# A new written-out order and three deeper rings in a fused retention and SoLU kernel

## The chip, the core and the metric

The kernel runs on one core of a Trainium2 chip. The metric is the device time of one execution in microseconds, and smaller is better. The kernel before took 209.02 us (median of three runs, 208.08 to 209.44). One further execution was recorded by the profiler; every duration below comes from it.

The core has five engines, each with its own queue that works strictly in order: TensorE (PE, matrix products and transposes), VectorE (DVE), ScalarE (ACT), GpSimd (POOL) and SyncE (SP, which here only issues transfers). They wait for each other through semaphores.

## What is computed

```
scores = (1/8) * q @ k^T                        # 8 batches, 8 heads, 576 positions, 64 wide
Dmat   = gamma[h] ** (i - j) where i >= j, else 0   # gamma[h] = 1 - 2**(-5-h)
ret    = (scores * Dmat) @ v
x      = ret, heads side by side                # 4608 tokens x 512
h      = x @ w_in                               # 512 -> 1024
u      = h * softmax(h)
ln     = (u - mean(u)) / sqrt(var(u) + 1e-6) * g_ln
out    = ln @ w_out                             # 1024 -> 512
```

All inputs and the output are float32; the products are taken in float16 with float32 sums.

## The kernel before

**Tiling.** Positions are cut into chunks of 128 tokens. A unit is a pair of chunks of one batch, loaded together (units 0 to 3, 5 to 8 and so on), or the two 64-token tails of two batches (units 4, 9, 14, 19). There are 20 units and 36 chunks. Within a unit the retention is computed directly; across chunks a 64 x 64 state per head is carried, decayed by `gamma ** 128`. The last chunk (35) is worked in two halves, `35.0` and `35.1`.

**Steps.** Each step of the work is a small function with a name, and one list, `PLAN`, writes out all of them in order. A word such as `xT:4@s` is step `xT` for chunk 4 on engine `s` (ACT; `v` is DVE, `g` is POOL), and `TL:2/05` is step `TL` for unit 2 into PSUM banks 0 and 5. `follow(PLAN)` issues the instructions word by word; so the list sets the order on every engine, and data and buffer conflicts only add waits. There are eight PSUM banks, and a bank may be written again when its reader is done.

The steps, by engine:

- SP: `lq`, `lk`, `lv` load a unit (512 KB each, 256 KB for the tails in two transfers); `wi`, `wo` load a quarter of `w_in` or `w_out`; `mt` a mask; `dT` transposes a chunk's `u` by a transfer; `st` stores a chunk.
- POOL: `q` and `v` scale by decay tables and cast; `s32` decays the state; `w2`, `pow` end the variance; and `k`, `s16`, `ws`, `osb`, `cwA`, `cwB` where the list says `g`.
- PE: `TL` transposes q and k of a unit, `sc` the scores, `kp` the state update, `xs` and `xv` the two parts of the retention's output, `mm1` and `mm2` the two dense products, `TU` and `lp` turn `u` where `dT` doesn't, `mean` a column mean of the scaled `w_out`; `tick` and `warm` are filler products on zeros.
- DVE: `m` masks scores, `max` and `solu` the row maximum and `u`, `t` the state, `cw` the centred `w_out`, `ox` a correction of the first six chunks; and copies where the list says `v`.
- ACT: `exp`, `sq` (the sum of squares), `w1`; and copies where the list says `s`.
- Copies out of PSUM: `eX` and `eY` (q and k turned), `eU`, `uX`, `uY` (`u` turned), `xT` (the retention's output turned and cast), `osb` (the scaled result).

**Order of the dependences.** Per unit: `lq`, `lk` -> `q`, `k` -> `TL` -> `eX`, `eY` -> `sc` -> `m` -> `xv` (with `v`) -> `xT`. Per chunk: `xT` -> `mm1` -> `max` -> `exp` -> `solu` -> (`sq`, and `dT` or `TU`) -> `mm2` -> `osb` -> `st`. Every `mm2` needs the scaled weights: `wo` -> `ws` for chunks 0 to 5, which use `w_raw16`, and `ws` -> `mean` -> `cw` for the rest, which use `w_out16`.

**Rings.** Buffers are used in turn, chunk n taking place n modulo the depth: `LB` = 3 units of loads, `XB` places for `xT`, `EB` for `e`, `UB` for `u`, `OB` for results, `UTB` for `u` turned by `dT` (chunks 10 to 33). Some places lie in room that has had its first use: the float32 copy of `w_out`, `w_out32`, which `ws` and `cw` read, holds the `dT` places.

```
ut_ = [w_out32[:, i].bitcast(F16).rearrange("p (c m) -> p c m", m=P) for i in range(UTB)]
o_sb = ring(min(OB, 5), [DM], FP, "o_sb")
o_sb += [w_out32[:, 6]] * (OB - len(o_sb))
u_ += [w_out32[:, 7].bitcast(F16)] * (UB - len(u_))
```

Ahead of `follow` the kernel loads the small tables on ACT's queue, writes zeros, ones, the identity and triangles, and builds two masks of 128 x 1024, the first on DVE and the second on POOL (both at line 865).

Of the kernel before, what the change touches and what calls it, by code (L numbers as in the profile page):

```python
# [43 lines left out]
def kernel(  # L44
# [690 lines left out]
    def warm(k, j, eng, bk):  # L735
# [26 lines left out]
        sc:4.0/01 exp:6 t:9 mm1:7/34 m:4.0 s32:9 lv:7 sq:5 lk:8 solu:6 q:6.0 lv:9 TU:2/01  # L762
        s16:5.0@s xv:4.0/2 eU:2.0@s t:10 q:6.1 lq:8 sc:5.0/67 xs:8/2 m:5.0 eU:2.1@s pow:0
        TL:6/50 xT:8@s max:7 q:7.1 eY:6@s sc:5.1/12 mm1:8/67 m:5.1 s16:9.0@g exp:7 s16:9.1@g
        osb:1@g eX:6@s solu:7 xv:5.1/10 xv:5.0/10 k:7.1@g xs:10/0 xT:9@s osb:0@g max:8
        sc:6.1/45 xT:10@s sc:6.0/12 k:7.0@g s16:10.0@s xs:12/3 mm2:2/0 m:6.0 sq:4 q:7.0 st:0
        st:1 k:8.0@g m:6.1 lk:10 sq:7 mm1:9/12 lk:9 v:8.1 ox:2 exp:8 lq:10 v:7.1 lq:9
        xv:6.1/03 osb:2@s max:9 xv:6.0/03 q:8.0 mm2:4/4 xT:12@s xT:11@s solu:8 s32:10 st:2
        exp:9 TU:3/03 ox:4 s16:10.1@g sq:8 mm1:10/67 v:9.0 solu:9 k:8.1@s v:8.0 lv:12 eU:3.0@v
        sq:6 TL:7/24 max:10 v:7.0 mm1:11/01 w1:3 sq:9 eU:3.1@v q:8.1 eX:7@v eY:7@s k:10.1@g  # L770
        lq:11 max:11 kp:7/23 kp:8/23 exp:10 lv:10 w2:3 mm2:5/5 k:9.0@g t:13 w1:6 lk:12 solu:10
        s16:13.0@s w2:6 lk:11 q:9.0 exp:11 TL:8/24 lv:11 ox:5 mm1:12/67 s32:13 lq:12 solu:11
        w1:9 eY:8@s q:10.1 eX:8@s t:14 sc:7.0/45 TU:4/01 m:7.0 s16:13.1@g mm2:6/3 eU:4.1@s
        pow:3 max:12 sq:11 q:10.0 sc:7.1/45 eU:4.0@v pow:6 xs:13/2 exp:12 mm2:7/1 m:7.1
        osb:5@g k:12.0@s k:10.0@g solu:12 osb:6@s osb:4@g xv:7.1/20 xv:7.0/20 sc:8.0/45
        osb:7@v osb:3@g xT:13@s sc:8.1/67 xs:14/0 m:8.1 mm1:13/23 xT:14@s st:4 sq:10 st:5 st:3
        m:8.0 lk:13 k:12.1@s TL:9/10 st:6 w2:9 TL:10/76 eX:9@v eY:9@s dT:11 q:11.0 xv:8.0/45
        eX:10@v sq:12 xv:8.1/45 mm1:14/01 max:13 q:12.0 dT:12 k:11.1@s v:12.0 exp:13 xs:15/4
        st:7 xs:16/5 max:14 mm2:8/7 v:10.1 dT:10 s16:14.1@s xT:15@v xT:16@s s16:14.0@g exp:14
        solu:13 mm1:15/45 q:12.1 eY:10@s solu:14 v:11.1 osb:8@s TL:12/23 max:15 pow:9  # L780
        sc:9.0/01 eX:12@s mm1:16/67 v:11.0 st:8 m:9.0 k:11.0@s lq:15 eY:12@s q:11.1 xv:9.0/0
        max:16 exp:15 sc:10.0/12 v:10.0 lq:14 xs:17/0 mm2:11/3 m:10.0 exp:16 lv:13 lq:13
        solu:15 xT:17@s dT:13 kp:11/21 kp:10/21 sq:14 t:18 sc:10.1/45 mm2:10/0 m:10.1 osb:11@s
        s32:18 sq:13 solu:16 s16:18.0@g st:11 TL:11/23 osb:10@s dT:15 xv:10.1/45 t:19 w1:12
        xv:10.0/45 eY:11@s sc:12.1/67 w2:12 eX:11@v mm1:17/01 s16:18.1@g lk:15 xT:18@s m:12.1
        s16:19.1@g sq:15 st:10 sc:11.0/67 max:17 sc:11.1/34 mm2:9/2 q:13.0 lk:14 m:11.1 exp:17
        k:13.0@g dT:14 m:11.0 xs:19/5 mm1:18/34 s16:19.0@g xT:19@s v:13.0 osb:9@s solu:17
        lv:14 k:13.1@s pow:12 xv:11.0/67 max:18 xv:11.1/67 mm1:19/01 q:14.0 st:9 exp:18 q:13.1
        xs:21/7 mm2:12/2 max:19 xT:21@s v:12.1 xT:20@s solu:18 v:13.1 exp:19 mm1:20/67
        k:15.1@g lv:16 osb:12@s solu:19 dT:16 k:14.0@g sq:16 TL:13/25 max:20 sc:12.0/01 st:12  # L790
        eX:13@s q:15.1 mm1:21/34 lq:17 m:12.0 lv:15 exp:20 v:14.0 eY:13@v xs:22/1 w1:15 sq:17
        mm2:14/0 max:21 w2:15 solu:20 exp:21 mm2:13/2 q:15.0 osb:14@v k:15.0@g solu:21 pow:15
        TL:15/60 osb:13@s st:14 xv:12.1/17 s32:19 eY:15@v xv:12.0/17 dT:18 sc:13.0/23 xT:22@s
        eX:15@v kp:13/45 sq:18 kp:12/45 m:13.0 sc:13.1/01 st:13 mm2:15/6 dT:17 sq:21 t:22
        m:13.1 s16:22.1@g lk:16 w1:18 mm1:22/23 sq:20 lk:17 s16:22.0@g osb:15@v dT:19 s32:22
        xs:23/7 xs:25/1 max:22 v:15.0 xT:23@s xv:13.1/41 st:15 xv:13.0/41 xs:24/4 mm1:23/67
        q:17.1 xT:25@v exp:22 t:23 v:16.1 xT:24@v sq:19 mm2:16/5 max:23 q:17.0 solu:22 v:16.0
        exp:23 mm1:24/01 dT:20 k:16.1@g osb:16@s solu:23 w2:18 sq:22 lq:16 mm1:25/34 k:16.0@g
        max:24 pow:18 st:16 lq:18 v:15.1 exp:24 mm2:17/2 max:25 k:17.0@g s16:23.1@g solu:24
        exp:25 kp:16/56 k:17.1@g kp:15/56 mm2:18/7 s16:23.0@g t:27 osb:17@s sq:23 solu:25  # L800
        s16:27.1@g s32:27 st:17 TL:17/02 osb:18@v TL:14/31 eX:17@s sc:15.1/45 t:28 q:16.1
        mm2:19/7 m:15.1 eX:14@s st:18 q:16.0 eY:14@s lk:18 s16:27.0@s eY:17@v sc:15.0/56 dT:23
        sc:14.0/34 m:15.0 TL:16/12 mm2:20/0 eY:16@s q:18.1 dT:22 eX:16@v osb:19@s m:14.0 lv:17
        sc:17.0/67 osb:20@s xv:15.1/15 xv:15.0/15 sc:16.0/23 xT:27@s xv:14.0/4 m:16.0 xs:26/4
        k:18.1@g sq:25 xs:28/5 st:20 mm1:27/01 dT:21 m:17.0 w1:21 xT:26@s w2:21 sq:24 q:18.0
        lv:18 mm1:26/23 max:27 lk:19 xT:28@s s32:28 exp:27 mm2:23/4 pow:21 max:26 solu:27
        exp:26 v:17.0 mm1:28/67 k:18.0@g osb:23@s solu:26 v:17.1 TL:18/05 max:28 sc:17.1/34
# [95 lines left out]
```

## Time and profile before

| | |
|---|---|
| median of three runs | 209.02 us |
| the profiled execution | 206.33 us, of which the span of its instructions is 204.6 us |
| busy share of the span | PE 96%, DVE 84%, ACT 79%, POOL 69% |
| transfers | 48.83 MB, 239 GB/s on average |
| PE filler (`warm`) | 56 products of 512 columns, 16.1 us busy |

An engine's busy time is the union of its instructions, without the issuing of transfers and without waits. PE's products are pipelined: one of 512 columns is shown as some 379 ns long, while the next may start sooner. PEld is PE's loading of the stationary operand, which overlaps with products. A row of groups reads: line, engine, operation, out<-in, shapes, count | busy us, mean ns of one | idle time before, and what ended it. A row of the timeline or of the chain begins with the start in us from the beginning of the span and the length. Lines are those of the kernel: L152 and L154 are the helper behind all copies, L195 that behind `q` and `v`, L467 that of all wide products, L227 of all transposes on PE, L345 is `sc`, L373 `kp`, L416 `xv`, L399 `xs`.

### The profile page before, as it was taken

How to read it: one execution, taken by the hardware profiler on the slowest of the kernel's cores; microseconds unless marked ns; L12 is line 12 of the kernel's file. 1: busy time of each engine (PE TensorE's matmuls, PEld its weight loads, DVE VectorE, ACT ScalarE, POOL GpSimd, SP SyncE). 2: the span in 40 equal slices, each digit the busy share in tenths (PEclk: the TensorE clock that was granted, in tenths of full speed). 3: DMA queues.
4: the chain of work that ended last, by engine and by line, in shares of the span. 5: the costliest groups of instructions: out<-in, count | busy, mean ns of one | idle time of the engine just before them, and what ended most of it. 6: DMA issues, size and time to landing. Idle time of an engine off the chain costs nothing.

```text
span 204.6 us, 7473 instructions
## 1 busy us (share of the span) xinstructions
PE 196.2 (96%) x3156; PEld 104.5 (51%) x3156; DVE 172.7 (84%) x225; ACT 162.0 (79%) x282; POOL 142.0 (69%) x196
## 2 busy tenths in 40 slices
...
GB/s 131 288 319 379 318 341 313 248 282 234 263 287 283 263 230 301 306 268 232 201 231 234 240 217 278 236 216 292 252 242 248 202 192 57 193 185 81 205 139 117
DMA packets 96369, 48.83 MB, mean 239 GB/s; under 512 B 40784, under 2 KB 90320, under 8 KB 96336
## 3 DMA queue, kind: packets, MB, share of 16 engines
...
q14 instruction: 9, 0.07, 0.1%
...
## 4 chain that ended last, share of the span: by engine, by line
PE 61%; POOL 9%; DMA 8%; DVE 8%; SPq 6%; ACT 4%; issue 3%; POOLq 0%; DVEq 0%; ACTq 0%
PE ps L467 47%; DMA qf<-in_q_dram 6%; SPq L174 4%; PE ps L345 4%; PE ps L416 3%; PE ps L227 3%; POOL v L195 3%; DMA w_out<-u 3%; PE ps L399 2%; POOL w_raw L704 2%; POOL q L195 2%; DVE w_out L722 2%; DVE u L539 2%; PE ps L373 2%; SPq L672 1%
## 5 line engine op out<-in xcount | busy, mean ns | idle before, releaser
L467 PE MATMUL ps<-w_in,xT 128*128 128x512 f16 x288 | 67.2, 379 | 0.3 <-DVE u L539 0.3
L496 DVE TENSOR_REDUCE col_nm<-ps 128x1 f32<-128x1024 f32 (+1 forms) x37 | 44.1, 1193 | 6.2 <-PE ps L467 5.9
L506 ACT ACTIVATE e<-ps,col_nm 128x1024 f32<-128x1024 f32 (+1 forms) x37 | 40.4, 1092 | 9.8 <-DVE col_nm L496 9.0
L539 DVE SCALAR_TENSOR_TENSOR u<-ps,e 128x1024 f16<-128x1024 f32 (+1 forms) x37 | 43.9, 1190 | 3.1 <-ACT e L506 1.7
L467 PE MATMUL ps<-w_out,w_out 128*128 128x512 f16 x192 | 44.9, 380 | 0.0
L467 PEld LDWEIGHTS <-xT 128*128 128x128 f16 x288 | 26.7, 98 | 30.8 <-ACT xT L152 0.3
L195 POOL TENSOR_TENSOR q<-qf,small 128x512 f16<-128x512 f32 x36 | 37.4, 1048 | 7.0 <-DMA qf<-in_q_dram 4.9
L547 ACT ACTIVATE e<-u,col_su 128x1024 f32<-128x1024 f16 (+1 forms) x37 | 41.5, 1124 | 0.0
L195 POOL TENSOR_TENSOR v<-vf,small 128x512 f16<-128x512 f32 x36 | 37.2, 1048 | 4.9 <-DMA vf<-in_v_dram 4.8
L355 DVE TENSOR_TENSOR ret<-ps,masks 128x1024 f16<-128x1024 f32 x22 | 26.5, 1218 | 9.0 <-PE ps L345 8.9
L467 PEld LDWEIGHTS <-w_out 128*128 128x128 f16 x192 | 17.8, 98 | 19.6
L152 ACT COPY tt<-ps 128x1024 f16<-128x1024 f16 (+1 forms) x23 | 20.6, 921 | 3.2 <-PE ps L227 2.2
L152 ACT CAST xT<-ps 128x512 f16<-128x512 f32 x28 | 15.9, 584 | 7.9 <-PE ps L399 4.9
L556 POOL TENSOR_SCALAR col_w<-col_ss 128x3 f32<-128x3 f32 (+1 forms) x14 | 2.7, 196 | 27.2 <-ACT col_w L533 13.4
L737 PE MATMUL ps<-zeros 128*128 128x512 f16 x56 | 16.1, 431 | 0.8 <-ACT tu L152 0.8
L154 POOL CAST s<-t 64x512 f16<-64x512 f32 x20 | 12.1, 608 | 4.8 <-DVE t L433 3.9
L446 POOL TENSOR_TENSOR s<-t,small 128x512 f32<-128x512 f32 x12 | 12.5, 1044 | 3.7 <-DVE t L431 3.5
L648 DVE TENSOR_SCALAR o_sb<-ps,col_rs 128x512 f32<-128x512 f32 (+1 forms) x14 | 10.0, 711 | 5.2 <-PE ps L467 2.7
L152 ACT CAST k<-kf 128x512 f16<-128x512 f32 x15 | 9.1, 621 | 6.3 <-DMA kf<-in_k_dram 6.3
L154 POOL CAST k<-kf 128x512 f16<-128x512 f32 x21 | 12.7, 611 | 1.6 <-DMA kf<-in_k_dram 1.6
L652 ACT ACTIVATE o_sb<-ps,col_rs 128x512 f32<-128x512 f32 x17 | 11.6, 685 | 1.4 <-PE ps L467 1.2
L355 DVE TENSOR_TENSOR w_in<-ps,masks 128x1024 f16<-128x1024 f32 x10 | 12.0, 1215 | 0.0
...
## 6 DMA issues: line engine op xcount, KB each, us to landing
...
out_dram<-o_sb SPq DMA_DIRECT2D x32, 256.0 KB, 3.4
...
qf<-in_q_dram SPq DMA_DIRECT2D x8, 128.0 KB, 4.2
kf<-in_k_dram SPq DMA_DIRECT2D x8, 128.0 KB, 4.7
```

The source lines that it names most:

```text
L152: nc.scalar.copy(out=out, in_=in_)
L154: {"v": nc.vector, "g": nc.gpsimd}[eng].tensor_copy(out=out, in_=in_)
L195: nc.gpsimd.tensor_tensor(out=out, in0=in_, in1=table.unsqueeze(2).to_broadcast([P, H, D]), op=ALU.mult)
L355: nc.vector.tensor_tensor(out=ret[u % RB][:, s], in0=bank(b0, 1024).rearrange("p (h w) -> p h w", w=P), in1=mk, op=ALU.mult,)
L446: nc.gpsimd.tensor_tensor(out=st32[c % 2].rearrange(flat), in0=T_OF[n].rearrange(flat), in1=gs2.unsqueeze(2).to_broadcast([P, 8, D]), op=A ...
L467: nc.tensor.matmul(out=o, lhsT=lhs(slice(0, P)), rhs=rhs, start=start, stop=stop)
L496: nc.vector.tensor_reduce(out=col("nm", n, j), in_=h(n, j), axis=AX.X, op=ALU.max, negate=True)
L506: nc.scalar.activation(out=e_[n % EB][:, part(j)], in_=h(n, j), func=ACT.Exp, bias=col("nm", n), accum_out=col("s", n, j),)
L539: nc.vector.scalar_tensor_tensor(out=u_[n % UB][:, part(j)], in0=h(n, j), scalar=1.0, in1=e_[n % EB][:, part(j)], op0=ALU.mult, op1=ALU.mu ...
L547: nc.scalar.activation(out=e_[n % EB][:, part(j)], in_=u_[n % UB][:, part(j)], func=ACT.Square, bias=col("su", n), scale=-1.0 * DFF, accum ...
L652: nc.scalar.activation(out=dst, in_=o, func=ACT.Copy, scale=col("rs", n))
L737: nc.tensor.matmul(out=bank(bk[0]), lhsT=zeros[:, 0:P], rhs=zeros, start=True, stop=True)
```

## The change

Four things change. First, the rings: `XB` goes from 3 to 5, `OB` from 5 to 6 and `UTB` from 4 to 6; `UB` stays 6, but one of its places moves into `w_out32[:, 7]`, and the sixth result place is `w_out32[:, 6]`. Second, seven tables `gn` that no step reads are left out of `small`. Third, the second mask is built on DVE instead of POOL. Fourth, `PLAN` is a new list: the same steps apart from filler (`tick` 12 to 6, `warm` 56 products to 52), in another order on every engine and in the transfer queue, with other banks, and with copies moved between engines. Counted over both lists:

| copies | ACT | DVE | POOL |
|---|---|---|---|
| `xT` | 28 to 23 | 8 to 13 | |
| `eX`, `eY` | 28 to 28 | 12 to 12 | |
| `eU` | 8 to 10 | 4 to 2 | |
| `osb` | 18 to 17 | 14 to 15 | 5 to 5 |
| `uX`, `uY` | 3 to 1 | 1 to 3 | |
| `ws` | 2 to 4 | | 6 to 4 |
| `k` | 15 to 16 | | 21 to 20 |
| `s16` | 12 to 13 | | 20 to 19 |

The transfer queue begins, before and after:

```
lq0 lk0 lq1 lv1 lk1 lv0 wi3 wi0 wi2 wi1 lk2 lq2 wo1 lq3 lk3 wo0 wo3 wo2 lv2 lv3
wi0 lq1 lk1 lq0 lk0 lv1 lv0 wi2 wi1 wi3 wo0 wo3 lq2 wo2 lk2 wo1 lq3 lk3 lv2 lv3
```

The diff, with most of both lists left out:

```diff
@@ -30,8 +30,7 @@
     gs = ge ** 128.0
 
     gm = np.broadcast_to((g ** -128.0).reshape(4, 2).T.reshape(1, 8), (P, 8))
-    gn = [ge ** float(2**i) for i in range(7)]
-    return np.concatenate([gq, gqt, gv, gvt, gs, gs, gm] + gn, axis=1).astype(np.float32)
+    return np.concatenate([gq, gqt, gv, gvt, gs, gs, gm], axis=1).astype(np.float32)
 
 
 def _np_tail_mask():
@@ -84,12 +83,12 @@
         return chunks[units[u]][1] == 4
 
 
-    LB, QB, KB, TB, WB, RB, XB, EB, UB, OB, TQ, UTB = 3, 2, 4, 4, 3, 3, 3, 4, 6, 5, 2, 4
+    LB, QB, KB, TB, WB, RB, XB, EB, UB, OB, TQ, UTB = 3, 2, 4, 4, 3, 3, 5, 4, 6, 6, 2, 6
 
     def ring(count, shape, dtype, name):
         return [const.tile([P] + shape, dtype, name=f"{name}{i}") for i in range(count)]
 
-    small = const.tile([P, 92], FP, name="small")
+    small = const.tile([P, 64], FP, name="small")
     tris = const.tile([P, 3, 64], FP, name="tris")
     masks = const.tile([P, 2, H, P], FP, name="masks")
     mask_t = const.tile([P, P], FP, name="mask_t")
@@ -124,7 +123,7 @@
     st32 = ring(2, [2, 4, D], FP, "s32_")
     xT_ = ring(XB, [4, P], F16, "xT")
     e_ = ring(EB, [DFF], FP, "e")
-    u_ = ring(min(UB, 6), [DFF], F16, "u")
+    u_ = ring(min(UB, 5), [DFF], F16, "u")
 
     ut_ = [w_out32[:, i].bitcast(F16).rearrange("p (c m) -> p c m", m=P) for i in range(UTB)]
     o_sb = ring(min(OB, 5), [DM], FP, "o_sb")
@@ -740,90 +739,89 @@
 
 
     PLAN = """
-        lq:0 lk:0 lq:1 lv:1 lk:1 tick:12/4 warm:18/4 lv:0 q:0.0 wi:3 q:0.1 k:0.0@s k:0.1@s
-        TL:0/62 wi:0 warm:8/4 q:1.1 eX:0@s eY:0@s wi:2 v:1.0 sc:0.0/01 sc:0.1/67 warm:9/4
-        m:0.1 q:1.0 wi:1 k:1.1@s m:0.0 v:1.1 k:1.0@s TL:1/67 lk:2 warm:5/4 v:0.1 eX:1@v eY:1@v
-        lq:2 v:0.0 sc:1.1/12 cwA:3@s kp:1/63 m:1.1 cwB:3@g kp:0/63 wo:1 xv:0.1/50 warm:1/4
-        cwA:0@s cwB:0@g t:0 sc:1.0/12 xv:0.0/50 warm:7/4 m:1.0 lq:3 s16:0.1@s cwB:2@s cwA:2@g
-        xT:0@v s16:0.0@s lk:3 xv:1.0/15 xv:1.1/15 cwB:1@s cwA:1@g xs:1/0 xT:2@v xs:3/5 s32:0
-        xT:1@s mm1:0/67 wo:0 g32 t:1 k:2.1@g mm1:1/12 s32:1 max:0 xT:3@s wo:3 s16:1.1@s
-        k:2.0@s q:2.1 mm1:3/34 exp:0 max:1 wo:2 q:2.0 solu:0 exp:1 ws:2@g TL:2/05 lv:2 max:3
-        eX:2@s mm1:2/67 ws:3@g eY:2@s solu:1 q:3.1 lv:3 warm:2/0 exp:3 max:2 q:3.0 TU:0/25
-        sc:2.1/01 lq:4 eU:0.1@s s16:1.0@g solu:3 k:3.1@g k:3.0@s warm:1/5 lk:5 exp:2 ws:0@g
-        m:2.1 TL:3/35 warm:2/4 ws:7@g eX:3@s solu:2 sc:2.0/01 lk:4 warm:3/4 eY:3@s ws:6@g
-        m:2.0 TU:1/34 ws:4@s ws:5@g sc:3.0/67 lq:5 ws:1@s eU:1.0@v sc:3.1/01 xs:4/5 v:2.1
-        m:3.1 eU:0.0@s mean/3 eU:1.1@s v:2.0 m:3.0 mm2:0/1 evm cw:4 v:3.1 sq:3 cw:2 v:3.0
-        kp:2/42 sq:1 ox:0 xv:3.1/67 xv:2.1/50 xv:2.0/50 cw:0 q:4.0 lv:6 kp:3/42 sq:0 xv:3.0/67
-        lk:6 xs:6/6 t:4 mm2:3/1 lv:5 cw:3 s16:4.1@g s16:4.0@s lv:4 cw:5 xT:4@s s32:4 xT:6@s
-        cw:7 xs:7/7 mt:0 xs:5/0 sq:2 mm1:4/45 k:5.0@g ox:3 k:4.0@g cw:1 xT:5@s q:5.1 lq:6
-        k:5.1@s t:5 mm1:5/01 xT:7@s max:4 q:5.0 w1:0 lk:7 v:6.1 cw:6 exp:4 TL:5/62 max:5
-        mm2:1/3 s16:5.1@g eX:5@s v:6.0 solu:4 lq:7 exp:5 mm1:6/67 k:6.0@g ox:1 eY:5@s v:5.1
-        solu:5 k:6.1@s TL:4/34 v:5.0 max:6 kp:6/25 eY:4@s eX:4@s w2:0 lv:8 kp:5/25 v:4.0
...
-        pow:34 mm2:32/6 exp:35.0 solu:35.1 pow:33 osb:30@s solu:35.0 sadd:35 w1:35 TU:5/02
-        osb:32@v lp:35.1/47 lp:35.0/35 eU:5.0@s mm2:33/1 suadd:35 st:32 eU:5.1@s uY:35.0@v
-        st:30 uX:35.1@s sq:35.0 mm2:34/5 sq:35.1 osb:33@v uX:35.0@s st:33 ssadd:35 uY:35.1@s
-        w2:35 mm2:35.0/2 pow:35 osb:34@v mm2:35.1/3 st:34 osb:35.0@v st:35.0 osb:35.1@v
-        st:35.1
+        wi:0 lq:1 tick:6/1 warm:28/1 lk:1 lq:0 lk:0 lv:1 lv:0 q:1.0 wi:2 k:1.0@s q:1.1 k:1.1@s
+        wi:1 TL:1/56 warm:8/1 q:0.1 eX:1@s eY:1@s cwB:0@g wi:3 cwA:0@g k:0.0@s sc:1.0/56 q:0.0
+        warm:5/1 k:0.1@s m:1.0 wo:0 v:1.0 sc:1.1/67 TL:0/50 m:1.1 warm:5/1 eX:0@s v:1.1 wo:3
+        eY:0@v v:0.0 sc:0.1/56 sc:0.0/34 lq:2 warm:4/7 m:0.1 v:0.1 cwA:2@s m:0.0 kp:1/52 wo:2
+        cwB:2@g kp:0/52 warm:2/7 g32 cwA:1@s t:0 xv:1.1/31 cwB:1@s xv:0.0/06 lk:2 xv:1.0/31
+        s16:0.1@s s16:0.0@g xv:0.1/06 xT:2@v cwB:3@s cwA:3@g xs:3/1 xT:0@v xs:1/6 wo:1 s32:0
+        mm1:2/45 ws:0@s ws:1@g t:1 xT:1@s lq:3 mm1:0/23 max:2 ws:6@s xT:3@s lk:3 exp:2
+        mm1:1/01 max:0 q:2.0 s16:1.0@s lv:2 q:2.1 solu:2 mm1:3/67 ws:4@s ws:5@g exp:0 max:1
+        lv:3 k:2.0@s k:2.1@g max:3 exp:1 ws:7@g TL:2/45 lq:5 solu:0 ws:3@g ws:2@s exp:3 solu:1
+        s32:1 lk:5 mean/3 eX:2@s solu:3 s16:1.1@g eY:2@s q:3.0 lk:4 TU:0/14 cw:4 eU:0.1@s
+        q:3.1 eU:0.0@v TU:1/52 sc:2.0/67 cw:0 sc:2.1/01 sq:3 k:3.0@g lq:4 mm2:0/4 m:2.0
+        k:3.1@g evm v:2.1 cw:1 eU:1.0@s TL:3/76 m:2.1 v:2.0 mm2:1/5 eX:3@s ox:0 lv:5 eY:3@s
+        v:3.1 cw:7 xs:4/4 eU:1.1@s ox:1 v:3.0 sc:3.0/67 xv:2.0/41 xv:2.1/41 m:3.0 xT:4@s q:5.0
+        lv:6 kp:2/20 kp:3/20 sq:0 sc:3.1/45 lk:6 cw:6 mm1:4/67 lv:4 t:4 k:5.0@s k:5.1@g m:3.1
+        s16:4.1@s s16:4.0@g lq:6 sq:2 s32:4 xs:5/1 mm2:3/2 max:4 xT:5@s q:4.0 cw:3 w1:0 exp:4
+        xs:6/5 t:5 xs:7/4 q:5.1 lq:7 xv:3.1/54 cw:2 sq:1 xv:3.0/54 mm1:5/01 s16:5.0@g solu:4
+        mt:0 xT:7@s v:5.0 xT:6@s cw:5 sq:4 v:5.1 mm1:6/67 max:5 lq:8 v:6.1 k:4.0@s ox:3 exp:5
+        lk:7 max:6 k:6.0@g TL:4/23 mm1:7/45 k:6.1@g eY:4@s solu:5 v:6.0 exp:6 lv:8 s16:5.1@g
+        eX:4@v TL:5/10 sq:5 solu:6 w2:0 kp:6/23 kp:5/23 q:6.0 eX:5@s t:9 sc:4.0/67 v:4.0 m:4.0
+        eY:5@s TU:2/12 q:6.1 eU:2.0@s max:7 xv:4.0/0 sc:5.0/67 xs:8/0 s32:9 lq:9 m:5.0 xT:8@s
+        exp:7 TL:6/01 s16:9.1@g lk:8 t:10 mm1:8/67 lv:9 q:7.1 eY:6@s solu:7 lv:7 pow:0
+        eU:2.1@s sc:5.1/34 k:7.1@g max:8 mm2:2/5 s16:9.0@s k:7.0@g eX:6@s q:8.1 m:5.1 exp:8
+        TU:3/10 osb:0@g ox:2 sc:6.0/34 eU:3.0@s q:7.0 m:6.0 xv:5.0/25 xv:5.1/25 xs:10/5 st:0
...
+        sq:12 mm2:11/2 eX:11@v dT:14 v:10.1 m:10.1 exp:16 mm2:10/0 v:12.1 eY:11@s solu:16
...
+        lq:16 v:16.0 solu:22 mm1:25/67 sq:20 dT:20 v:14.0 max:23 mm1:24/12 k:17.1@g max:25
...
+        osb:22@s solu:27 s16:31.1@s s16:31.0@g t:32 TL:18/56 q:19.0 dT:27 sc:17.1/01 eX:18@v
...
+        xT:33@v xT:34@s solu:29 s16:32.1@s mm2:26/3 w1:27 s16:32.0@s max:30 dT:29 sq:29
...
+        solu:33 dT:31 sq:30 mm1:34/01 max:32 st:25 eY:19@s exp:32 mm2:28/2 max:34 solu:32
...
+        mm2:31/5 eU:5.0@v xT:35@s w2:33 st:27 eU:5.1@s pow:30 mm1:35.0/0 st:29 dT:30
+        mm1:35.1/7 osb:31@s max:35.0 mm2:32/6 st:28 max:35.1 st:31 nmm:35 exp:35.0 mm2:33/4
+        exp:35.1 osb:32@v solu:35.0 sadd:35 st:32 pow:33 w1:35 solu:35.1 mm2:34/5 w2:34
+        osb:33@v pow:34 suadd:35 st:33 sq:35.0 lp:35.0/62 lp:35.1/40 osb:34@v sq:35.1 mm2:30/1
+        uX:35.0@v st:34 uY:35.0@s uY:35.1@v ssadd:35 uX:35.1@v w2:35 pow:35 mm2:35.1/3
+        osb:30@s mm2:35.0/0 st:30 osb:35.1@v st:35.1 osb:35.0@v st:35.0
...
             )
 
         make_mask(nc.vector, masks[:, 0], tris[:, 1:3], P)
-        make_mask(nc.gpsimd, masks[:, 1], tris[:, 0:2], P)
+        make_mask(nc.vector, masks[:, 1], tris[:, 0:2], P)
         follow(PLAN)
```

109 lines of the change are left out of this document (49 added, 60 removed).

## The prediction

> **What bounds the kernel now.** I read the page first, then busy time by stage, then the chain of waits, and last the rows of single operations.
>
> ```profile
> span 204.6 us, 7473 instructions
> PE 196.2 (96%) x3156; PEld 104.5 (51%) x3156; DVE 172.7 (84%) x225; ACT 162.0 (79%) x282; POOL 142.0 (69%) x196
> ```
>
> The profiled execution took 206.33 us, 1.7 around its span; the median of the runs, 209.02, is 2.7 above that. Three engines are near full, so the stages have to tell them apart (columns: window, wall time, then PE, PEld, DVE, ACT, POOL busy).
>
> ```profile
> 0.00:22.00 22.00, 19.81 (x325) 10.16 (x326) 10.50 (x15) 9.18 (x14) 15.45 (x25) 1.00 1.00 280
> 22.00:42.00 20.00, 18.58 (x384) 10.15 (x382) 18.09 (x23) 18.32 (x28) 18.96 (x21) 1.00 1.07 304
> 42.00:148.00 106.00, 105.08 (x1864) 56.87 (x1866) 101.28 (x129) 93.96 (x162) 87.54 (x115) 1.00 1.07 254
> 148.00:176.00 28.00, 27.94 (x433) 15.13 (x422) 25.08 (x31) 23.42 (x43) 14.37 (x22) 1.00 0.91 190
> 176.00:201.00 25.00, 24.76 (x173) 12.20 (x170) 17.40 (x30) 17.17 (x39) 5.63 (x15) 1.00 0.67 156
> ```
>
> Up to 22 us the loads rule (PE is busy there mostly with filler on zeros). From 22 to 42 DVE, ACT and POOL are each over 90% busy. From 42 to 148 DVE is idle 4.7 of 106 us and PE 0.9. After 176 DVE has 7.6 us to spare and PE none. The chain of waits gives PE's true pace (start, length, what):
>
> ```profile
> 12.86 11.95 DMA qf<-in_q_dram
> ...
> 66.60 0.57 PE ps L416 x32
> ...
> 73.92 0.71 PE ps L373 x64
> 74.63 1.83 PE ps L467 x8
> 76.46 0.57 PE ps L227 x32
> 77.04 1.83 PE ps L467 x8
> 78.87 0.35 PE ps L345 x16
> ...
> 130.29 8.63 PE ps L467 x40
> ...
> 195.45 5.32 PE ps L467 x32
> ```
>
> Wide matmuls follow each other at 8.63/40 = 0.216 us; so a step of eight (`mm1`, `mm2`, `mean`) is 1.73 us; `TL` and `TU` are 0.57, `sc` 0.35, two `kp` 0.71, two `xv` 0.57, all at most. With the shortest common length of each kind the list holds 171.6 us of PE work without filler, in either plan: the steps are the same.
>
> ```profile
> 8.21 0.68 PE L227 MATMUL ps<-ident,q 64*128 64x64 f16 x16
> ```
>
> PE's real work runs from this row to 200.8, so 21 us of that stretch are holes or filler; step by step, some 12 of them lie after 20 us.
>
> **The change, part by part.**
>
> *Work moved between engines.* I counted each copy by engine in both lists.
>
> ```profile
> L152 ACT CAST xT<-ps 128x512 f16<-128x512 f32 x28 | 15.9, 584 | 7.9 <-PE ps L399 4.9 <-PE ps L467 1.4 <-PE ps L416 1.3
> L154 DVE CAST xT<-ps 128x512 f16<-128x512 f32 x8 | 5.5, 682 | 0.7 <-PE ps L416 0.7
> L152 ACT COPY tt<-ps 128x1024 f16<-128x1024 f16 x18 | 17.9, 1013 | 3.2 <-PE ps L227 2.2 <-DVE u L539 1.0
> L154 DVE COPY tt<-ps 128x1024 f16<-128x1024 f16 x6 | 4.0, 685 | 0.4 <-PE ps L227 0.3
> L648 DVE TENSOR_SCALAR o_sb<-ps,col_rs 128x512 f32<-128x512 f32 x12 | 9.0, 749 | 4.6 <-PE ps L467 2.1 <-issue 1.4 <-POOL col_rs L565 0.9
> L704 POOL TENSOR_TENSOR w_raw<-w_out,g 128x512 f16<-128x512 f32 x6 | 6.1, 1036 | 0.0
> L865 POOL TENSOR_TENSOR masks<-tris,small 128x1024 f32<-128x1024 f32 x1 | 2.9, 2936 | 0.8 <-DMA small<-small_c 0.8
> L865 DVE TENSOR_TENSOR masks<-tris,small 128x1024 f32<-128x1024 f32 x1 | 1.2, 1226 | 1.0 <-DMA small<-small_c 1.0
> ```
> ```profile
> L154 DVE COPY w_in<-ps 128x256 f16<-128x256 f16 x1 | 0.3, 285 | 0.0
> ```
> ```profile
> 11.91 2.35 DVE L355 TENSOR_TENSOR ret<-ps,masks 128x1024 f16<-128x1024 f32 x2 [7.22 <-PE ps L345]
> ```
>
> DVE gains five `xT` (5 x 0.68 = 3.4), one `osb` (0.75) and two of the last chunk's small copies (2 x 0.285), and loses about 0.8 on `eX`/`eY` (three full ones become three of half size) and 1.7 on `eU` (two fewer): +2.2 us. The second mask adds 1.2, but at about 5 us, inside the 7.2 us that DVE waits for PE before 11.91. ACT gets two `ws`, more full evictions and fewer `xT`: about +2.1. POOL loses two `ws` (2.1), the mask (2.9), one `k` and one `s16` (0.6 each): -6.2, and most of this lies before 40 us, where POOL carries the chain.
>
> Where do the 2.2 us of DVE lie? With these durations summed in list order, at PE work 20 the new list has DVE at 25.6 (old 27.9), at 50 at 63, at 90 at 104, at 120 at 134 (old 63, 104.5, 135). Only beyond 141 us of PE work (about 169 us of the old run) does the new list have more left, 27 against 25. There the last two rows of the stages show DVE idle 10 us; so the term is **0**. Without that cover it would be +2.2.
>
> *The order of the loads.* The old queue begins q0, k0, q1, v1, k1, v0, then the four `wi`; the new one wi0, q1, k1, q0, k0, v1, v0, then three `wi`. The rows of the first users show the pace:
>
> ```profile
> 9.38 1.05 POOL L195 TENSOR_TENSOR q<-qf,small 128x512 f16<-128x512 f32 x1 [0.92 <-DMA qf<-in_q_dram]
> ...
> 12.95 1.14 ACT L152 CAST k<-kf 128x512 f16<-128x512 f32 x2 [1.86 <-DMA kf<-in_k_dram]
> ...
> 21.29 0.62 ACT L152 CAST w_in<-w_in 128x512 f16<-128x512 f32 x1 [0.17 <-DMA w_in<-in_moe_w_in_dram]
> ...
> 28.11 1.89 PE L467 MATMUL ps<-w_in,xT 128*128 128x512 f16 x8 [0.30 <-DVE u L539]
> ```
>
> Between 9.38 (q1) and 12.95 (k1) two loads came: 1.8 us each; between the last `wi` (21.29) and q2 (in at 12.86 + 11.95 = 24.81, by the chain) k2 and q2. A `w` load of the same size, in longer rows, I take at 1.35 us, the gap between the last two `wi` arrivals; bounds 1.3 and 1.8. Ten loads stand before the first `mm1` in both orders, so `mm1` starts near 22.3 (old 21.9) and the four run to 29.2. q2 was load 12; the new order has k2 as load 15, with wo0, wo3 and wo2 in addition: 24.8 + 3 x 1.35 = 28.9 (to 30.2 by the upper bound). One cast of 0.6 behind it, `TL:2` starts at 29.6 and ends at 30.2; in the old run the same PE work was done at 29.8 (28.11 + 1.73). **+0.4**. The smaller table `small` (92 to 64 columns) saves nothing: the mask that it feeds has slack.
>
> *From 30 to 56 us.* q3 and k3 land some 4 us later than before. Between `TL:2` and `TL:3` the new list has `mean`, two `TU`, `mm2:0` and two `sc`: 1.74 + 1.14 + 1.73 + 0.65 = 5.3 us of PE work, which is what hides them; uncovered they cost up to 4. I followed the queues by hand with the row durations; three rows of the old run fix what to compare with.
>
> ```profile
> 36.09 4.07 POOL L195 TENSOR_TENSOR v<-vf,small 128x512 f16<-128x512 f32 x4
> ```
> ```profile
> 54.33 1.22 DVE L355 TENSOR_TENSOR ret<-ps,mask_t 128x1024 f16<-128x1024 f32 x1
> ```
> ```profile
> 56.31 0.41 PE L416 MATMUL ps<-ret,v 128*64 128x128 f16 x8
> ```
>
> POOL: last `ws` at 31.4 (with wo1, load 16), q3 at 35.0, k3 at 36.2, `v:3.0` done at 40.2 (old 40.1). PE: `mean` 31.5, `TU:0` 33.2, `mm2:0` 35.4, `TL:3` 37.1, `mm1:4` 41.2, with 21.2 us of work done, about a microsecond ahead of the old run. But DVE has done less in exchange, and takes over as the pace: it starts `m:4.0` at 54.8 with 41.6 done (old 54.33, 40.6). PE then waits near 54 for `m:4.0` and `eY:5`, and issues `xv:4.0` at 56.0 with 33.3 done; old: 56.31 with 33.4. With the 0.4 above included, the whole start is **-0.2**.
>
> *56 us to the end.* PE has 137.4 us left in both lists, DVE about the same until 141. For each stretch of 10 us of PE work I took the busiest engine's sum. From PE work 40 on these sums come to 133.7 against 133.2 in the old list; with stretches of 7, equal; with 5, 0.3 less. **0**, between -2 and +2 by where the cuts fall.
>
> *The extra places.* UTB goes from 4 to 6, XB 3 to 5, OB 5 to 6; `u` keeps six.
>
> ```profile
> L619 SPq DMA_TRANSPOSE w_out<-u x24: 1232/1376/4132, 88.2 to 188.0; - x24
> ...
> DMA to landing us min/median/max: 3.0/4.8/7.7
> ```
> ```profile
> out_dram<-o_sb SPq DMA_DIRECT2D x32, 256.0 KB, 3.4
> ```
> ```profile
> DVE u L539 <- DMA out_dram<-o_sb: 0.8, 1, 0.8
> ...
> DVE u L539 <- DMA w_out<-u: 0.4, 1, 0.4
> ```
>
> In the new order `dT` 14, 20, 27, 29 and 31 stand ahead of the `mm2` that would free a fourth place, so five of 24 use the room; of the `xT` two near the end do; no result needs its sixth place, as the store five before it stands at least 3.5 us ahead and a store lands in about 3.4. The named waits on these transfers amount to 1.2 us on DVE; PE feels perhaps a quarter: **-0.3**, between 0 and -1.2. The new places lie in `w_out` parts whose last `cw` I put near 40 to 48 us, before their first use. `dT:27` stands 0.7 us ahead of the end of `solu:27`; SP then holds `st:22`, `dT:26` and `lv:19`, the last with 7 us in hand. From `dT` to `mm2` the new list leaves 5.2 us or more (old 3.5), so the 4.8 us landing is covered at least as well.
>
> Sum: -0.2 + 0 + 0 - 0.3 = -0.5: span 204.1, profiled execution 205.8, median **208.5**. The forecast is no change that can be measured; about 1% (2 us) is what a measurement of this kernel tells from none.
>
> **The rivals.**
>
> *A: holes close (faster).* DVE was idle 1.9 us in 22 to 42 and 4.7 in 42 to 148. If the new order, with 130 bank reuses right behind their reader instead of 146 of 282, closes half: -3.3, so 205.7. For it: the new list has no filler between `TL:2` and the end, where the old has eight, in four places. Against it: the sums by stretch leave only about 2 us between old list and old run after 28 us. Chance 0.32.
>
> *B: DVE is the bound (slower).* If DVE sets the end even after 148 us, its 2.2 us count in full, and the 0.4 of the late k2 stays: +2.6, 211.6. It decides from the point where PE waits for `solu` and `osb` in the last 50 us. Against it: DVE's 7.6 idle us after 176. Chance 0.19. By the Trainium skill (Perfetto Trace Analysis, "Identifying the Most-Contended Engine") matmul busy time says little, and the share of LDWEIGHTS is the better measure; by it PE would be at 51% and DVE at 84% the contended engine. The trace disagrees for the late stages: forty matmuls 0.216 us apart leave PE no room.
>
> *C: the late q3 and k3 are not hidden (slower).* If `mean` or `mm2:0` wait too (the last `ws` hangs on load 16), up to 4 us come back: 212.9. Against it: 5.3 us of cover. Chance 0.07.
>
> **How the numbers follow.** No change 0.42, A 0.32, B 0.19, C 0.07. Its own range is 206.5 to 210.5 (the ±2 of the sums). To reach both sides: 205.0 to 212.0 leaves out the rest of A below and most of C above. Faster by over 1%: 0.33; within: 0.42; slower: 0.25.
>
> **What would show it.** Right: `TL:2` near 29.6, `mm1:4` near 41, `xv:4.0` near 56, DVE busy over 95% from 42 to 148, PE ending within 1 us of 200.3, DVE idle 5 us or more after 176. Wrong: filler-like gaps on PE before `TL:3` (C), PE waiting for DVE after 150 (B), or `xv:4.0` before 54 (A).

## The result and the profile after

The changed kernel took 209.75 us in the median of 20 runs (207.96 to 211.41), the kernel before 207.85 in 20 runs of its own (206.14 to 211.33): a ratio of **1.0094, interval 1.0068 to 1.0119**. It is slower by about 1.9 us, where -0.5 had been forecast. Ratios leave out executions more than 1.5% above the fastest of their kernel; in before_nofill below that is five of 12 runs, so the median of all twelve stands beside its ratio.

The profiled execution took 210.44 us with a span of 208.4. That is 4.1 more than the profiled execution of before, over twice the difference of the medians: the one of before was among its kernel's fastest runs, this one lies above its kernel's median. The page and the stages (same columns as before; the last stage is longer because the run is):

```profile
span 208.4 us, 7449 instructions
...
PE 196.1 (94%) x3146; PEld 104.4 (50%) x3146; DVE 175.3 (84%) x232; ACT 165.1 (79%) x280; POOL 135.9 (65%) x191
```
```profile
0.00:22.00 22.00, 19.33 (x321) 9.72 (x322) 11.00 (x15) 9.33 (x13) 13.46 (x26) 1.00 1.00 292
22.00:42.00 20.00, 18.19 (x273) 9.75 (x271) 17.17 (x24) 17.66 (x27) 17.68 (x20) 0.91 1.12 288
42.00:148.00 106.00, 102.95 (x1884) 56.19 (x1880) 100.21 (x129) 96.27 (x163) 83.97 (x109) 1.00 1.10 249
148.00:176.00 28.00, 26.96 (x478) 14.74 (x475) 24.28 (x30) 22.72 (x39) 14.50 (x21) 1.00 1.07 205
176.00:205.00 29.00, 28.63 (x202) 14.00 (x200) 22.49 (x40) 19.15 (x41) 6.33 (x17) 1.00 0.61 144
```

Three things differ from before. The granted clock in 22 to 42 is 0.91. PE, which was idle 0.9 us in 42 to 148 and 0.06 in 148 to 176, now is idle 3.05 and 1.04. DVE still has 3.7 and 6.5 us to spare in the last two stages.

The waits of PE (us in total, times, longest) have two lines at the top that were no terms of before: there the first stood at 0.3 us, and no PE wait for a transpose was listed.

```profile
PE ps L466 <- DVE u L538: 1.8, 1, 1.8
PE ps L466 <- DMA w_out<-u: 1.7, 2, 0.9
```

The first lies ahead of `mean`. In the timeline (start, length, what, in brackets the idle time before it) PE has nothing between the end of `TL:2` at 29.85 and 31.63, and then the weights of `mean` are loaded 0.42 us apart:

```profile
29.44 0.41 PE L226 MATMUL ps<-ident,k 64*128 64x64 f16 x16
31.63 2.88 PE L466 MATMUL ps<-w_raw,ones 128*128 128x512 f16 x8 [1.78 <-DVE u L538]
34.44 1.70 PE L226 MATMUL ps<-ident,u 64*128 64x64 f16 x64
```
```profile
32.60 0.15 PEld L466 LDWEIGHTS <-ones 128*128 128x128 f16 x1 [0.22 <-issue]
33.02 0.15 PEld L466 LDWEIGHTS <-ones 128*128 128x128 f16 x1 [0.28 <-issue]
33.45 0.15 PEld L466 LDWEIGHTS <-ones 128*128 128x128 f16 x1 [0.27 <-issue]
```

The second line is two `mm2` steps that wait for their turned `u` (18 and 21). SP's rows are the two transfers, from issue; the chain of waits gives issue to landing; PE's rows are the steps that wanted them:

```profile
131.69 1.84 SPq L618 DMA_TRANSPOSE w_out<-u  x1
...
148.79 3.64 SPq L618 DMA_TRANSPOSE w_out<-u  x1
```
```profile
131.69 6.11 DMA w_out<-u
137.84 5.35 PE ps L466 x24
147.34 1.34 SPq L173
148.79 7.98 DMA w_out<-u
156.82 1.90 PE ps L466 x8
```
```profile
137.84 1.47 PE L466 MATMUL ps<-w_out,w_out 128*128 128x512 f16 x6 [0.76 <-DMA w_out<-u]
...
153.98 1.90 PE L466 MATMUL ps<-w_in,xT 128*128 128x512 f16 x8
156.82 1.47 PE L466 MATMUL ps<-w_out,w_out 128*128 128x512 f16 x6 [0.93 <-DMA w_out<-u]
```

Followed step by step (time from the start of one PE step to the next, less the shortest of its kind), the 3.9 us that PE ends later than before (204.6 against 200.8) arise as follows: 1.4 before 60 us, 0.2 from 60 to 120, 2.0 from 120 to 160, 0.3 behind it.

### The profile page after: what moved, and what is told of

It reads as the page before. It is cut to its first block, busy times and chain, and to the rows that moved or that the text cites. A ratio compares the mean times of both kernels' runs of the same rounds, so it can differ in the third digit from the quotient of the medians.

```text
span 208.4 us, 7449 instructions
## 1 busy us (share of the span) xinstructions
PE 196.1 (94%) x3146; PEld 104.4 (50%) x3146; DVE 175.3 (84%) x232; ACT 165.1 (79%) x280; POOL 135.9 (65%) x191
## 4 chain that ended last, share of the span: by engine, by line
PE 62%; DMA 11%; DVE 10%; ACT 6%; SPq 6%; POOL 1%; issue 1%
PE ps L466 48%; DMA w_out<-u 7%; SPq L173 5%; PE ps L226 4%; DMA w_in<-in_moe_w_in_dram 4%; PE ps L344 3%; DVE col_nm L495 3%; PE ps L415 3%; PE ps L398 3%; DVE u L538 2%; ACT e L505 2%; ACT w_in L151 2%; DVE ret L354 2%; PE ps L372 1%; ACT tt L151 1%
## 5 line engine op out<-in xcount | busy, mean ns | idle before, releaser
L194 POOL TENSOR_TENSOR v<-vf,small 128x512 f16<-128x512 f32 x36 | 37.1, 1046 | 5.0 <-DMA vf<-in_v_dram 4.9
L538 DVE SCALAR_TENSOR_TENSOR u<-ps,e 128x1024 f16<-128x1024 f32 x30 | 36.4, 1219 | 1.8 <-ACT e L505 1.3
L546 ACT ACTIVATE e<-u,col_su 128x1024 f32<-128x1024 f16 x30 | 34.4, 1149 | 0.1
L151 ACT COPY tt<-ps 128x1024 f16<-128x1024 f16 (+1 forms) x21 | 20.0, 971 | 5.0 <-PE ps L226 5.0
L151 ACT CAST xT<-ps 128x512 f16<-128x512 f32 x23 | 13.1, 584 | 3.6 <-PE ps L415 2.3
L153 POOL CAST s<-t 64x512 f16<-64x512 f32 x19 | 11.5, 606 | 4.4 <-DVE t L432 2.6
L736 PE MATMUL ps<-zeros 128*128 128x512 f16 x52 | 14.0, 420 | 0.0
L651 ACT ACTIVATE o_sb<-ps,col_rs 128x512 f32<-128x512 f32 x14 | 9.6, 684 | 4.2 <-PE ps L466 1.5
L153 POOL CAST k<-kf 128x512 f16<-128x512 f32 x20 | 12.0, 610 | 0.1
L344 PE MATMUL ps<-tt 64*64 64x128 f16 (+1 forms) x408 | 11.3, 220 | 0.5 <-DVE u L538 0.2
```

Source lines behind the costliest of these rows:

```text
L151: nc.scalar.copy(out=out, in_=in_)
L153: {"v": nc.vector, "g": nc.gpsimd}[eng].tensor_copy(out=out, in_=in_)
L194: nc.gpsimd.tensor_tensor(out=out, in0=in_, in1=table.unsqueeze(2).to_broadcast([P, H, D]), op=ALU.mult)
L344: nc.tensor.matmul(out=bank(bk[e])[ii, hp * P : (hp + 1) * P], lhsT=keys(u, i, hp, s)[dd], rhs=queries(u, i, hp)[dd], start=True, stop=True,)
L538: nc.vector.scalar_tensor_tensor(out=u_[n % UB][:, part(j)], in0=h(n, j), scalar=1.0, in1=e_[n % EB][:, part(j)], op0=ALU.mult, op1=ALU.mu ...
L546: nc.scalar.activation(out=e_[n % EB][:, part(j)], in_=u_[n % UB][:, part(j)], func=ACT.Square, bias=col("su", n), scale=-1.0 * DFF, accum ...
```

## The experiments

The theories that the expectations name: **S**, the loss arises in the start (up to some 58 us); **C**, more narrowly, the idle time ahead of `mean` lets the granted clock fall; **T**, PE waits for late transposes; **D**, DVE's added copies count after all (the prediction's rival B). S2 is the start being late whatever the clock.

**Splicing the two orders, and moving transfers.** Four kernels on one chip.

```
old_start: words of the old list up to pow:0 (ahead of TL:6), then what is left of the new list in its order
old_rest:  words of the new list up to TL:6, then what is left of the old list in its order
```
```diff
 room_only: the kernel before, old list
-XB, OB, UTB = 3, 5, 4     ring(min(UB, 6), ...)
+XB, OB, UTB = 5, 6, 6     ring(min(UB, 5), ...)
 dt_early: the changed kernel
-... lq:17 dT:16 ... dT:17 dT:18 ... lv:18 lv:17 ... lk:18 dT:21 ...
+... lq:17 dT:18 ... dT:17 dT:16 ... dT:21 lv:18 lv:17 ... lk:18 ...
```

> The order of before up to the turn of unit 6 (some 57 us), from there the changed order; the added places and the second mask on DVE stay. Theory S (the loss arises in the start: PE stands 1.95 us ahead of mean at 29.7, mean then takes 2.81 us, and xv:4.0 came at 57.9 where the kernel before had 56.3): 1.4 to 1.6 us come back, 208.2 to 208.4, a ratio near 1.002. Theory T (the loss arises late: PE waits for dT:18 at 135 and for dT:21 at 154, about 2 us in the trace): nothing comes back, 209.8, ratio 1.009. Theory D (DVE's 2.2 us of added copies count): nearly nothing comes back, 209.5, since the added copies xT and osb lie after 57 us.

> The changed order up to the turn of unit 6 (some 58 us), from there the order of before; the added places stay. Theory S: the loss stays, 209.3 to 209.5, ratio 1.007. Theory T: the loss is gone, 207.9, ratio 1.000. Theory D: 208.0 to 208.2, since DVE has its old copies from 58 us on.

Measured: old_start 212.18 us, ratio 1.0237 (1.0207 to 1.0266); old_rest 212.71, 1.0261 (1.0210 to 1.0313). No theory had this, and neither settles where the loss arises, because the splice itself costs more than what was sought. The waits of each around the splice (old_rest from 57 to 66 us, then old_start from 57 to 76):

```profile
DVE w_in L354 <- PE ps L344: 3.0, 1, 3.0
PE ps L344 <- ACT tt L151: 2.3, 1, 2.3
```
```profile
POOL q L194 <- DMA qf<-in_q_dram: 6.1, 1, 6.1
PEld L226 <- POOL q L194: 2.9, 3, 1.8
```

In old_rest the scores of unit 5 take a bank that the other list's ACT clears late; in old_start the loads of the second list come too late for the first. In both splices the banks and loads of one list did not fit the order of the other.

> The kernel before with nothing but the added places (XB 5, OB 6, UTB 6, the sixth u in w_out), in its own order. All theories: at most the 1.2 us that DVE was seen waiting for stores and transposes, of which PE feels a quarter; 207.5 to 207.9, ratio 0.998 to 1.000. Over 1.003 would mean that the places themselves cost something (for example xT and result copies that run ahead and crowd an engine).

Measured: 207.88 us, 1.0014 (0.9982 to 1.0046). The places alone neither help nor hurt by what can be measured.

> The changed kernel with dT:16 and dT:18 exchanged on SP's queue, and dT:21 ahead of lv:18 and lv:17. Theory T: both transposes land before mm2:18 and mm2:21 want them, PE's waits of 0.9 and 1.1 us and what follows from them go, 207.8 to 208.3, ratio 1.000 to 1.002. Theories S and D: 209.5 to 209.8, ratio 1.008 to 1.009.

Measured: 213.97 us, 1.0340 (1.0299 to 1.0382): some 4 us above the changed kernel's 209.75, against all three theories. The timeline of DVE says why:

```profile
136.86 1.23 DVE L538 SCALAR_TENSOR_TENSOR u<-ps,e 128x1024 f16<-128x1024 f32 x1 [4.09 <-DMA w_out<-u]
```

`solu:22` writes the place of `u` that chunk 16 held (six places), so it waits until `dT:16` has read it; the exchange made `dT:16` the late one, and `max`, `exp` and all of DVE stood behind it. A transpose has two readers of its time: `mm2` behind it, and `solu` six chunks on. The edit had looked at the first only. It says nothing against T; the next one leaves SP's queue alone.

**Covering the two places without moving a transfer.** Four kernels on the same chip as before.

```diff
 keep_clock: the changed kernel
-... ws:7@g TL:2/45 lq:5 ...
+... ws:7@g warm:7/4 TL:2/45 lq:5 ...
 land_later: the changed kernel
-mm1:24/12 ... mm2:18/0 ... mm2:16/5 ...     mm1:28/67 ... mm2:21/0 ... sc:16.1/45 ...
+mm1:24/12 ... mm2:16/5 ... mm2:18/0 ...     mm1:28/67 ... sc:16.1/45 mm2:21/0 ...
 both: the two together
 before_nofill: the kernel before
-TL:2/05 ... warm:2/0 ... warm:1/5 ... warm:2/4 ... warm:3/4 ...
+TL:2/05 ...
```

> The changed kernel with seven filler matmuls (1.5 us) ahead of TL:2, in a bank that is free then; TL:2 then runs at 30.6 to 31.2 instead of 29.1 to 29.8, and its reader eX:2 takes it at 32.1 either way. Theory C (PE's 1.9 idle us ahead of mean let the granted clock fall in about half of the runs, and mean's eight matmuls then take 2.8 us instead of 1.7): the granted clock reads 0.996 or more in every run, mean takes 1.75 us, mm1:4 stands near 42.2 instead of 43.3, and the median falls by 0.5 to 0.8 us, 208.8 to 209.3, ratio 1.004 to 1.006. Rival S2 (the start is late because of its loads and copies, whatever the clock): mean's pace changes nothing behind 42 us, where DVE sets the pace; 209.6, ratio 1.009.

> The changed kernel with two pairs exchanged in PE's order: mm2:16 ahead of mm2:18, and sc:16.1 ahead of mm2:21; no transfer is moved, so that solu waits for no transpose later than it did. Theory T (PE waits for dT:18 and dT:21): the wait of 0.9 us at 137 goes, the one of 1.1 us at 156 falls to 0.8, and m:16.1 starts 0.3 to 1 us sooner; 208.3 to 208.8, ratio 1.002 to 1.005. If DVE or ACT set the end there (theory D): 209.5 to 209.8.

> Both edits, the filler ahead of TL:2 and the two exchanges. Theories C and T together: 207.5 to 208.3, ratio 0.999 to 1.003, so that the loss is explained by these two places. If either gain is taken back by another engine: 208.8 or more.

> The kernel before without its eight fillers between TL:2 and TU:1 (29.8 to 35 us). Theory C: PE then stands idle for 0.5 to 0.9 us in four places within 5 us, the granted clock falls below 0.995 in a good part of the runs, and the median rises by 0.5 to 1.0 us, ratio 1.002 to 1.005. If the fillers only fill: ratio 0.998 to 1.001 and a clock of 1.0 as before.

Measured: keep_clock 208.59 us, 1.0041 (1.0006 to 1.0076); land_later 207.80, 1.0019 (0.9983 to 1.0054); both 207.66, **1.0003 (0.9970 to 1.0036)**; before_nofill 210.10, 1.0031 (0.9981 to 1.0081). In the profile of both (span 205.3) PE comes from `TL:2` to `mean` with 0.37 us of idle time, `mean` has full pace, and the second pair runs without a wait:

```profile
29.31 1.67 PE L736 MATMUL ps<-zeros 128*128 128x512 f16 x7
30.92 0.41 PE L226 MATMUL ps<-ident,q 64*128 64x64 f16 x16
31.16 0.40 PE L226 MATMUL ps<-ident,k 64*128 64x64 f16 x16
31.93 1.89 PE L466 MATMUL ps<-w_raw,ones 128*128 128x512 f16 x8 [0.37 <-DVE u L538]
```
```profile
153.89 0.42 PE L344 MATMUL ps<-tt 64*64 64x128 f16 x16
154.24 1.90 PE L466 MATMUL ps<-w_out,w_out 128*128 128x512 f16 x8
```

The clock is shown by before_nofill. Stages of 4 us (PE busy first, granted clock third from the end), from that kernel, then of the changed kernel, then of both:

```profile
32.00:36.00 4.00, 1.72 (x66) 1.46 (x67) 4.00 (x7) 4.00 (x7) 4.00 (x5) 0.79 1.15 292
36.00:40.00 4.00, 4.00 (x65) 2.43 (x60) 3.69 (x4) 3.10 (x5) 4.00 (x5) 0.50 0.98 247
```
```profile
28.00:32.00 4.00, 2.21 (x40) 1.19 (x39) 4.00 (x7) 4.00 (x7) 3.95 (x5) 1.00 1.17 300
32.00:36.00 4.00, 4.00 (x72) 2.21 (x69) 3.10 (x6) 2.48 (x5) 3.85 (x6) 0.57 1.11 274
```
```profile
28.00:32.00 4.00, 3.63 (x47) 1.86 (x46) 4.00 (x7) 4.00 (x8) 3.94 (x6) 1.00 1.17 305
32.00:36.00 4.00, 3.78 (x105) 2.34 (x105) 4.00 (x8) 4.00 (x6) 3.85 (x5) 1.00 1.10 277
```

In these rows the clock of the next 4 us is 0.50 or 0.57 where PE was busy about half of 4 us, and 1.00 where it was busy 90%. The half does not always bring the fall. In after_again, a further profile of the changed kernel, the clock stayed:

```profile
28.00:32.00 4.00, 2.19 (x40) 1.15 (x39) 4.00 (x7) 3.95 (x8) 3.96 (x6) 1.00 1.17 304
32.00:36.00 4.00, 3.85 (x105) 2.34 (x105) 4.00 (x9) 3.86 (x6) 3.85 (x5) 1.00 1.08 275
```

The mean granted clock of a run fell below 0.995 in 11 of 12 runs of before_nofill and in none of the 34 of the kernel before beside them. Over all kernels here that begin like the changed one without filler ahead of `TL:2`, it did so in 21 of 72 runs; over those with the filler, in none of 45. So the old list's eight fillers don't only fill: without them the clock falls. What that costs is less clear. The ratio of before_nofill is not clear of 1, while the median of all its runs is 2.6 us up.

**One exchange at a time, and DVE's copies.** Beside each other on a second chip: the changed kernel again, each half of land_later alone, and both with five late `xT` on ACT.

```diff
 only_18: -mm2:18/0 ... mm2:16/5   +mm2:16/5 ... mm2:18/0
 only_21: -mm2:21/0 ... sc:16.1/45 +sc:16.1/45 mm2:21/0
 copies_act (on top of both): -xT:27@v xT:29@v xT:31@v xT:32@v xT:33@v
                              +xT:27@s xT:29@s xT:31@s xT:32@s xT:33@s
```

> The changed kernel as it is, for its times and clocks on the same chip as the three beside it. All theories: ratio 1.007 to 1.012 to the kernel before; theory C: about half of the runs with a granted clock under 0.995, these about 0.9 us above the others; theory T: in the profile mm2:18 and mm2:21 wait for transposes again (0.4 to 1.1 us each).

> The changed kernel with mm2:16 ahead of mm2:18 in PE's order and nothing else. Theory T: the wait ahead of mm2:18 goes (0.4 to 0.9 us), the one ahead of mm2:21 stays; ratio 1.003 to 1.007. Theory D: as after_again.

> The changed kernel with sc:16.1 ahead of mm2:21 in PE's order and nothing else. Theory T: the wait ahead of mm2:21 (0.6 to 1.1 us) falls by the 0.35 us of sc:16.1, and m:16.1 starts sooner on DVE; the one ahead of mm2:18 stays; ratio 1.005 to 1.009. Theory D: as after_again.

> The kernel with both edits, and in addition xT 27, 29, 31, 32 and 33 on ACT instead of DVE: 3.4 us less on DVE after 150 us, 2.9 us more on ACT. Theory D (the copies added to DVE count): 1 to 2 us less than the kernel with both edits, 206 to 206.7, ratio 0.993 to 0.997. The step of the prediction that puts DVE's added work at nothing: 207.4 to 208.2, ratio 0.999 to 1.003; more if ACT, 80% busy there, is late with them.

Measured: after_again 209.22 us, 1.0068 (1.0038 to 1.0097); only_18 209.22, 1.0060 (1.0024 to 1.0095); only_21 209.80, 1.0078 (1.0043 to 1.0113); copies_act 208.11, 1.0030 (0.9992 to 1.0068). Either half alone is no gain that can be measured. Theory D falls: with 3.6 us less on DVE from 148 to 176 (the row is of copies_act; both had 25.43 us of DVE and 27.89 of PE there), PE is as busy as it was and the time is no shorter (D had expected a ratio of 0.993 to 0.997):

```profile
148.00:176.00 28.00, 27.90 (x485) 15.02 (x480) 21.84 (x26) 24.55 (x43) 14.86 (x23) 1.00 1.02 202
```

No run of after_again had a granted clock under 0.995, which C had expected in half of them, and it still was 0.7% slower. T had expected two waits for transposes in its profile, of 0.4 to 1.1 us each; there is one, of 0.22 us. So the fallen clock alone does not make the loss. The profile, of the fastest of the six runs, does not show all of what is left. With full clock the idle time ahead of `mean` is the same, and `mean` takes its full pace:

```profile
32.07 1.89 PE L466 MATMUL ps<-w_raw,ones 128*128 128x512 f16 x8 [1.88 <-DVE u L538]
...
136.89 5.35 PE L466 MATMUL ps<-w_out,w_out 128*128 128x512 f16 x24 [0.22 <-DMA w_out<-u]
```

The last four put the main kernels side by side on a third chip:

> The changed kernel on the same chip as the three beside it. All theories: ratio 1.006 to 1.012. Theory C needs a granted clock under 0.995 in some of the runs and these slower by about 0.9 us.

> mm2:16 ahead of mm2:18 and sc:16.1 ahead of mm2:21. Theory T: 0.7 to 1.5 us under after_b on this chip, ratio 1.001 to 1.005. If its earlier result was the chip's: within 0.4 us of after_b.

> The filler ahead of TL:2. Theory C: as far under after_b as the runs with a lowered clock lift that kernel's median, 0.3 to 0.9 us, and no run under 0.995. If idle ahead of mean costs nothing beyond the clock, the runs of after_b with full clock equal it within 0.4 us.

> Both edits. Theories C and T: ratio 0.997 to 1.003, 1.2 to 2 us under after_b. If the two together are not level with the kernel before on this chip, a third place holds the rest: 1.004 or more.

| kernel | us | ratio to before | interval | against after_b |
|---|---|---|---|---|
| after_b | 209.48 | 1.0094 | 1.0065 to 1.0123 | |
| land_later_b | 208.76 | 1.0082 | 1.0054 to 1.0110 | 0.7 us less |
| keep_clock_b | 208.62 | 1.0063 | 1.0035 to 1.0091 | 0.9 us less |
| both_b | 207.57 | 1.0007 | 0.9989 to 1.0026 | 1.9 us less |

The two edits together take off the whole loss, on two chips. On this one each alone takes off less than a microsecond; land_later_b, at 1.0082, lies outside the 1.001 to 1.005 that T had expected. On the first chip, where the changed kernel was not run beside them, land_later alone was nearly level with the kernel before (1.0019, against 1.0094 in the result). The shares of the two are not settled: on this chip the intervals of the single edits overlap that of the changed kernel, and keep_clock_b lies 0.9 us under after_b although only one of six runs of after_b had a fallen clock. What the filler brings beyond the clock stays open. Nor did an edit beat the kernel before: both is level with it.

The profile of after_b (span 207.6, full clock) shows a third late place, which no theory had: the load of q for unit 15, ahead of `TL:15`. POOL's `q` behind it starts at 125.96, where in the profile of both it starts at 123.89 (last row):

```profile
125.96 2.05 POOL L194 TENSOR_TENSOR q<-qf,small 128x512 f16<-128x512 f32 x2 [4.12 <-DMA qf<-in_q_dram]
128.07 0.38 PE L226 MATMUL ps<-ident,q 64*128 64x64 f16 x14 [0.48 <-POOL q L194]
137.68 5.35 PE L466 MATMUL ps<-w_out,w_out 128*128 128x512 f16 x24 [0.29 <-DMA w_out<-u]
156.07 1.90 PE L466 MATMUL ps<-w_out,w_out 128*128 128x512 f16 x8 [0.35 <-DMA w_out<-u]
```
```profile
123.89 2.06 POOL L194 TENSOR_TENSOR q<-qf,small 128x512 f16<-128x512 f32 x2 [2.58 <-DMA qf<-in_q_dram]
```

Compared by the starts of the `exp` steps, after_b is 0.3 us behind both_b at 124 us, 1.3 at 130 and 2.0 at 142, and stays there. So about half of what it loses arises at this load and most of the rest around `mm2:18`. In the profiles of both and both_b PE has no such wait, although neither edit touches this load; the first profile of the changed kernel has none either, so it varies from run to run. That the two edits together repair the loss is measured; that it arises at their two places alone is not.

## Why the prediction was wrong

**The bound and the cover of DVE: right.** DVE's +2.2 us at nothing stands: 3.7 and 6.5 us idle after 148, and copies_act. Rival B, the DVE bound, is out; PE waits after 150 us, but for transfers. DVE's share in 42 to 148 is 94.5%, not over 95.

**The loads: right.** `TL:2` was put at 29.6; it started at 29.11, 29.55 and 29.45 in three profiles of the changed kernel. Rival C (late q3 and k3) did not come; the filler-like gap ahead of `TL:3`, its sign, did, but it belongs to `mean`, which the prediction itself had at 31.5 behind a `TL:2` that ended at 30.2.

**30 to 56 us, -0.2: the first step that failed.** `mean` started at 31.63 as followed. Its price of 1.74 us was taken from a stretch in which PE had no gap; it took 2.88, and behind it all is late: `TU:0` 34.44 (forecast 33.2), `mm2:0` 36.6 (35.4), `TL:3` 38.5 (37.1), `mm1:4` 43.3 (41.2), `m:4.0` 56.5 (54.8), `xv:4.0` 57.85 (56.0; before 56.31). With full clock (after_again) `xv:4.0` is at 56.96 and `mm1:8` at 59.52 against 59.24 before: the term is +0.3 with full clock and +1.2 with a fallen one (`mm1:8` at 60.42). The clock had fallen in 11 of the first 20 runs, whose median is 210.2 against 209.3 for the other nine. The prediction had noted that the new list has no filler there, and had counted that as a gain (rival A).

**The extra places, -0.3: the second step that failed.** "So the 4.8 us landing is covered at least as well" set the smallest room (5.2 us) against the median landing, with the longest, 7.7, in the same row. The measured landings of 6.11 and 7.98 us left waits of 0.76 and 0.93; in two other profiles of the changed kernel the waits were 0.22 and none (after_again), 0.29 and 0.35 (after_b), so the size of this loss varies from run to run. The old list issued `dT:18` 16 us and `dT:21` 10.7 us ahead of its `mm2` (at 123.45 and 149.14 in the profile of before), the new one 5.4 and 7.1 us ahead of the time when PE was free for it (137.84 - 0.76 - 131.69, and 156.82 - 0.93 - 148.79). The room itself, put between 0 and -1.2, measured +0.3 us in the old order (-0.4 to +1.0 by the interval of room_only); in the new order it was not tested alone.

**56 us to the end, 0.** The stretch sums hold for 60 to 120 us (0.2 off). They can't see a landing, of a transpose or of a load such as q of unit 15, so the loss in 120 to 160 was outside of their kind, not in their ±2.

**The sum.** -0.5 had two terms with the wrong sign: +0.3 to +1.2 in place of -0.2, and in place of -0.3 a loss of up to 2.0, of which 0.2 to 1.7 was seen as waits for transposes. The range of 205 to 212 held the time because it was wide, and partly by luck: the 208.5 was reckoned from 209.02, and from the 207.85 of the 20 runs the same sum gives 207.35, 2.4 under the measured time. By the Trainium skill (TensorE: Matmul & The Clock Gate, "What's actually happening") the half clock comes after an idle window of about 3.4 us; here it came after 1.78 us of full idle in a stretch 55% busy, and did not come after 1.88 us in after_again, so the longest gap alone is no safe measure. The Trainium skill (the same page, "A second HAM failure mode: psum-queue depth-cycling") says that frequent small gaps do it too; before_nofill, with no gap over 1.3 us ahead of its fall, agrees.
